# A woven delta-rule attention and feed-forward kernel: weight casts, one weight conversion and the transposes of the first chain in another order

## The chip, the cores and the metric

The kernel runs on one core of one Trainium2 chip. The metric is device time in microseconds of one execution; three runs of the kernel before gave a median of 634.15 us (633.36 to 634.79). The engines are named as the profile names them: PE (TensorE, with PEld for its weight loads), DVE (VectorE), ACT (ScalarE), POOL (GpSimd) and SP (SyncE, which here only issues DMAs).

## The reference

Per batch and head (4 x 8 of them) a 48 x 48 state is carried over 768 steps; the output of the attention is read before the state is updated. All heads side by side make a 3072 x 384 input of a feed-forward layer.

```python
k_n = k / (np.linalg.norm(k, axis=-1, keepdims=True) + 1e-06)
for t in range(S):                       # S = 768, D = 48, 4 x 8 heads
    y[:, :, t] = einsum('bhd,bhde->bhe', q[:, :, t], state)
    v_old = einsum('bhde,bhd->bhe', state, k_n[:, :, t])
    state = state + beta * einsum('bhd,bhe->bhde', k_n[:, :, t], v[:, :, t] - v_old)
x = y.transpose(0, 2, 1, 3).reshape(B * S, H * D)      # 3072 x 384
h = x @ w_in                                           # 384 x 2048
out = np.maximum(0.01 * h, h) @ w_out                  # 2048 x 384
```

## The kernel before

The 768 steps are cut into 12 blocks of 64. Within a block the recurrence is solved as a triangular system. The grams of keys and queries (pg, L289) are made on PE and scattered through memory (gs, gd, L). Then `inv` eliminates column by column on DVE: a product into tmp (L370) and an update of T (L375) per column. T starts with a memset (L397) and ends with a copy on ACT (L435); it is then sent out in pieces td and tt (L442, L443), which come back as operands of two merge products on PE, sq for pz and pu (L470) and rt. After these come pk (L598), pw (L615), pc (L625), and py (L635), which is the block's output; ACT copies it to ys (L637). Two groups (g = 0, 1) cover the four sequences.

`columns(n)` transposes ys into 384 x 256 columns on PE (px, L668), three pieces cc of 128 rows, and splits each into a high part xh (ACT, L119) and a low part xl (DVE, L120). `ffn(n)` runs over 16 chunks f of the 2048 middle columns: nine products into ph (L697: xh and xl with the high weights, xh with the low ones), gh and the rectified ph on ACT (L702, L703), the low part gl on DVE (L705), and later six products po (L687). The chunks alternate between two banks of PSUM, so that ph of chunk f comes after gl of chunk f-2. When a block is done, ACT copies po to ob and SP issues the stores to out (L732).

The weights come in as packed integers and are converted during blocks 0 and 1: per chunk an absolute value on ACT (L144), a clamp (L146), L150, L151 and L152 on DVE, a cast of the high part on ACT (L156), and the low part either on DVE (L169) or as products wl on PE (L175, L176).

The work of a block's solve, the next block's inverse and the feed-forward layer are woven together in the code, and then a scheduler orders the instructions of each engine by its own modelled times. `behind(name)` adds one constraint to it: the instruction is issued after the one marked with that name. A constraint in block 0 can therefore move instructions of later blocks. Each engine, and each DMA queue, does its instructions in order.

Of the kernel before, what the change touches and what calls it, by code (L numbers as in the profile page):

```python
# [9 lines left out]
F32 = mybir.dt.float32  # L10
# [13 lines left out]
TB = NSEQ * C  # L24
GS = 2
NGR = NSEQ // GS
# [5 lines left out]
P = 128  # L32
# [14 lines left out]
def delta_moe_kernel(ctx: ExitStack, tc, kq0, kqT, kv, qT, beta, cst, w_all, out, nblk):  # L47
# [10 lines left out]
    nc = tc.nc  # L58
    NFC, _, DO = w_all.shape[1:]
    NCC = DO // P  # L60
# [7 lines left out]
    ps_a = ctx.enter_context(tc.tile_pool(name="ps_a", bufs=4, space=PSUM))  # L68
# [20 lines left out]
    def of(x, n, g):  # L89
        return ring[x][(n * NGR + g) % NR[x]]  # L90
# [21 lines left out]
    raws, mark = {}, {}  # L112

    def behind(name):

        return tc.issue_after(mark[name]) if name in mark else nullcontext()

    def split(src, hi, lo):
        mark["xh"] = nc.scalar.copy(hi, src).ins  # L119
        return nc.vector.tensor_tensor(lo, src, hi.bitcast(F32), ALU.subtract)  # L120

    def load_w(f, gate=None):
        if f < NFC:
            raws[f] = raw = sb.tile([P, 2 * DO], U64, tag=f"w{f}", name=f"wr{f}", bufs=1)
            if gate:
                with behind(gate):
                    nc.vector.memset(raw[:, 0:1].bitcast(F32), 0.0)
            with behind("kq"):
                nc.sync.dma_start(raw, w_all[:, f].rearrange("p x n -> p (x n)"))
# [4 lines left out]
    def weights():  # L134

        for f in range(NFC):
            words = raws.pop(f).bitcast(U32).rearrange("p (n two) -> p two n", two=2)
            lo, hi = words[:, 0], words[:, 1]  # L140
            g = sb.tile([P, 2 * DO], F32, tag=f"c{f % 4}", name=f"cg{f}", bufs=1)
            gi = g.bitcast(U32)
            with behind("S" if f < KA else "xh"):
                nc.scalar.activation(g, hi.bitcast(F32), AF.Abs)  # L144
            with behind("mask" if f < 2 else "conv" if f == 2 else "x" if f < KA else f"gl{f - AG}" if f"gl{f - AG}" in mark else "x"):
                i = nc.vector.tensor_scalar(g, g, HI_MIN, HI_MAX, ALU.max, ALU.min)  # L146
            mark["work"] = i.ins
            if f + WAHEAD >= WEARLY:
                load_w(f + WAHEAD, "work")
            nc.vector.tensor_scalar(gi, gi, 3, 0x3FFFFFF8, ALU.logical_shift_left, ALU.bitwise_and)  # L150
            nc.vector.scalar_tensor_tensor(gi, hi, 0xC0000000, gi, ALU.bitwise_and, ALU.bitwise_or)  # L151
            i = nc.vector.scalar_tensor_tensor(gi, lo, 29, gi, ALU.logical_shift_right, ALU.bitwise_or)  # L152
            mark["conv"] = i.ins
            t = sb.tile([P, 4 * DO], F32R, tag=f"w{f}", name=f"w{f}", bufs=1)
            with behind("rv" if f < 2 else "xh"):
                nc.scalar.copy(t[:, 0:2 * DO], g)  # L156
            later.append((f, g, t))
            for y in range(2):
                for x, w in enumerate((wi, wo)):
                    w[y][f] = t[:, (2 * y + x) * DO:(2 * y + x + 1) * DO]  # L160
            yield
# [18 lines left out]
    Lh, gm, nrm, Tts, zs, ys, xs, done = {}, {}, {}, {}, {}, {}, {}, set()  # L180

    def need(gen, fn, n):
        while (fn, n) not in done:
            next(gen)
# [379 lines left out]
    def solve(n):  # L564
# [19 lines left out]
        def quarters():  # L584

            return ((c, u, e) for u in range(GU) for c in range(2) for e in range(2))
# [42 lines left out]
        def step_y(g):  # L629

            qa, v = of("q", n, g), of("v", n, g)
            pv = ps_a.tile([P, 512], F32, tag="a", name=f"py{n}_{g}")
            for c, u, e in quarters():
                a = (c ^ (u // NPAIR)) * C + e * HC
                nc.tensor.matmul(pv[a:a + HC, u * D:(u + 1) * D], qa[:, c, u, e * HC:(e + 1) * HC], v[:, c, u], start=True, stop=True)  # L635
            ys[n, g] = y = sb.tile([P, DO], F32, tag="ys", name=f"ys{n}_{g}", bufs=3)
            mark["ys"] = nc.scalar.copy(y, pv[:, 0:DO]).ins  # L637

        stages = [(0, load), (1, tie), (LD, kt), (LD + 1, step_w), (LD + 2, step_y), (LD + 3, step_s)]
        if n in (0, nblk - 1):  # L640
# [19 lines left out]
    def columns(n):  # L660

        need(sv, solve, n)
        xs[n] = parts = []
        px = [ps_a.tile([P, 2, TB], F32, tag="a", name=f"px{n}_{i}") for i in range(2)]
        part = [px[cc // 2][:, cc % 2] for cc in range(NCC)]
        for cc, x in enumerate(part):
            for g in range(NGR):
                i = nc.tensor.transpose(x[:, g * P:(g + 1) * P], ys[n, g][:, cc * P:(cc + 1) * P], eye)  # L668
        mark["px"] = i.ins
        for cc, x in enumerate(part):  # L670
            xh, xl = (sb.tile([P, TB], F32R, tag=t, name=f"{t}{n}_{cc}", bufs=3) for t in ("xh", "xl"))
            i = split(x, xh, xl)
            if not n:
                mark["x"] = i.ins
            parts.append((xh, xl))

    def ffn(n):
# [35 lines left out]
        if n + 1 < nblk:  # L713
            columns(n + 1)
# [69 lines left out]
KA, KB, WB = 4, 2, 12  # L784
IV, GG = ((7, 17), (6, 17), (6, 17), (2, 17)), ((0, 2), (1, 2), (1, 2))
LL, AG = 2, 6
# [67 lines left out]
```

## Time and profile before

| | before |
|---|---|
| median of 3 runs (lowest to highest) | 634.15 us (633.36 to 634.79) |
| span of the profiled execution | 633.8 us |
| busy PE, DVE, ACT | 590.5, 442.4, 331.1 us |
| mean granted clock of PE | 0.983 |
| share of the chain that ended last: PE, DVE | 81%, 11% |

The span is what the profiler saw from the first to the last instruction of one execution. A row of a timeline gives the start, the duration, the engine, the line, the operation and its operands; in square brackets stands the idle time of that engine just before, and what released it. A row with a count is a run of equal instructions. Instructions of one engine overlap by some hundredths of a microsecond, so spacings are taken from starts.

### The profile page before, as it was taken

What the parts mean: (1) busy time and instruction counts of PE and PEld (TensorE: products, weight loads), DVE (VectorE), ACT (ScalarE), POOL (GpSimd) and SP (SyncE); (2) the same over time, 40 slices, a digit from 0 to 9 for tenths busy, and PEclk for the clock granted to TensorE, in tenths of its full rate; (3) what the DMA queues carried; (4) which work ended last, traced back from release to release, by engine and by line L of the source; (5) the groups of instructions that cost most, each with busy time, mean ns of one, the idle gap of its engine ahead of it and who ended that gap; (6) DMA issues with size and microseconds to landing.
All of it is one profiled execution on the core that took longest, in us unless ns stands there. A gap on an engine that the chain in (4) does not pass through costs nothing.

```text
span 633.8 us, 22738 instructions
## 1 busy us (share of the span) xinstructions
PE 590.5 (93%) x9244; PEld 547.0 (86%) x9244; DVE 442.4 (70%) x1996; ACT 331.1 (52%) x855; POOL 10.7 (2%) x17
## 2 busy tenths in 40 slices
PE   5277999999989989999999999999999999999996
PEld 4265898988879989999999999999999999999996
DVE  3999999998747958759759759659669569221211
ACT  3465998634636446545546545545555545544332
POOL 6000000000000000000000000000000000000000
PEclk9986999999989999999999999999999999999999
DMA  6982973153156561453462561552571440500101
GB/s 124 302 261 79 252 248 77 24 113 52 27 105 135 113 115 37 90 103 72 93 119 54 102 143 21 99 122 46 102 155 28 88 102 4 87 24 3 26 1 26
DMA packets 124585, 59.72 MB, mean 94 GB/s; under 512 B 111424, under 2 KB 114624, under 8 KB 124480
## 3 DMA queue, kind: packets, MB, share of 16 engines
q1 hardware_dynamic: 121728, 57.28, 40.6%
q8 instruction: 73, 1.20, 0.8%
q10 hardware_dynamic: 2752, 0.98, 0.8%
q14 instruction: 32, 0.26, 0.2%
HBM read 46.96 MB, written 11.27 MB: 92 GB/s over the span
## 4 chain that ended last, share of the span: by engine, by line
PE 81%; DVE 11%; DMA 3%; SPq 2%; issue 2%; ACT 1%; DVEq 0%; ACTq 0%
PE ph L697 32%; PE po L687 30%; PE pk L598 3%; PE pg L289 3%; PE pw L615 3%; PE pc L625 3%; PE py L635 2%; DVE T L375 2%; DVE tmp L370 2%; PE wl L175 1%; DMA tt<-T 1%; PE px L668 1%; DVE cg L152 1%; PE pz L470 1%; PE pu L470 1%
## 5 line engine op out<-in xcount | busy, mean ns | idle before, releaser
L697 PE MATMUL ph<-xh,w 128*128 128x256 f32 x1152 | 246.6, 290 | 2.9 <-DVE gl L705 2.0
L697 PEld LDWEIGHTS ph<-xh,w 128*128 128x128 f32 x1152 | 192.1, 191 | 12.1 <-DVE gl L705 3.7
L687 PE MATMUL po<-w,gh 128*128 128x384 f32 x768 | 188.4, 343 | 3.1 <-ACT gh L702 3.1
L705 DVE TENSOR_TENSOR gl<-ph,gh 128x256 fp32r<-128x256 f32 x192 | 80.8, 421 | 150.7 <-ACT ph L703 148.8
L697 PE MATMUL ph<-xl,w 128*128 128x256 f32 x576 | 163.7, 286 | 1.0 <-DVE xl L120 1.0
L702 ACT ACTIVATE gh<-ph 128x256 fp32r<-128x256 f32 x192 | 73.7, 384 | 157.6 <-PE ph L697 145.2
L687 PEld LDWEIGHTS po<-w,gh 128*128 128x128 f32 x768 | 132.7, 189 | 7.5 <-ACT gh L702 5.3
L687 PE MATMUL po<-w,gl 128*128 128x384 f32 x384 | 116.5, 339 | 0.0
L370 DVE TENSOR_TENSOR tmp<-T,L 128x60 f32<-128x60 f32 (+35 forms) x661 | 111.6, 207 | 1.0
L375 DVE TENSOR_TENSOR T<-T,tmp 128x60 f32<-128x60 f32 (+35 forms) x661 | 111.5, 206 | 0.8
L697 PEld LDWEIGHTS ph<-xl,w 128*128 128x128 f32 x576 | 109.8, 191 | 2.5 <-DVE xl L120 1.7
L703 ACT ACTIVATE ph<-ph 128x256 f32<-128x256 f32 x192 | 73.3, 382 | 0.0
L687 PEld LDWEIGHTS po<-w,gl 128*128 128x128 f32 x384 | 67.1, 189 | 0.3 <-issue 0.2
L600 ACT ACTIVATE rt<-pk 48x512 f32<-48x512 f32 x44 | 26.1, 593 | 24.9 <-PE pk L598 24.1
L306 DVE TENSOR_TENSOR rq<-pg,csb 64x256 f32<-64x256 f32 x80 | 33.8, 423 | 4.0 <-ACT gs L293 2.6
L617 ACT COPY rv<-pw 64x384 f32<-64x384 f32 x48 | 22.7, 473 | 12.7 <-PE pw L615 11.9
L627 ACT COPY rv<-pc 48x384 f32<-48x384 f32 x44 | 20.8, 474 | 10.6 <-PE pc L625 10.1
L606 DVE TENSOR_TENSOR rv<-rv,nt 64x384 f32<-64x384 f32 x44 | 22.3, 553 | 0.6
L289 PE MATMUL pg<-kq 48*64 48x128 f32 x640 | 22.7, 275 | 0.0
L615 PEld LDWEIGHTS pw<-rv,rt 128*32 128x32 f32 x1536 | 19.2, 115 | 4.1 <-ACT gh L702 2.2
L615 PE MATMUL pw<-rv,rt 128*32 128x48 f32 x1536 | 21.6, 213 | 0.6 <-issue 0.6
L635 PEld LDWEIGHTS py<-rv,rq 128*32 128x32 f32 x1536 | 18.4, 112 | 4.2 <-ACT ph L703 2.3
(96 smaller groups left out, 542.6 us busy)
## 6 DMA issues: line engine op xcount, KB each, us to landing
wr<-in_w_all SPq DMA_DIRECT2D x16, 768.0 KB, 7.7
kq<-in_kqT SPq DMA_DIRECT2D x40, 192.0 KB, 4.1
L<-gd SPq DMA_DIRECT2D x20, 256.0 KB, 4.2
rk<-in_kv SPq DMA_DIRECT2D x24, 192.0 KB, 3.4
rv<-in_kv SPq DMA_DIRECT2D x24, 192.0 KB, 3.9
rq<-in_qT SPq DMA_DIRECT2D x24, 192.0 KB, 3.7
out<-ob SPq DMA_DIRECT2D x46, 96.0 KB, 2.3
td<-T SPq DMA_DIRECT2D x40, 64.0 KB, 2.9
```

The source lines that it names most:

```text
L289: nc.tensor.matmul(ps[b][c * 64:(c + 1) * 64, p * 128:(p + 1) * 128], kq[r, c ^ b, p, 0], kq[r, c ^ b, p].rearrange("p x t -> p (x t)"), s ...
L306: nc.vector.tensor_tensor(qa[DN, c, b * NPAIR:(b + 1) * NPAIR], pv[b][r, 1], tri[r].rearrange("p (o t) -> p o t", o=1).broadcast_to([C, NP ...
L370: nc.vector.tensor_tensor(tv, t[:, :, j:j + 1].broadcast_to([P, k, w]), L[:, j, j + 1:].rearrange("p (o w) -> p o w", o=1).broadcast_to([P ...
L375: mark["steps"] = nc.vector.tensor_tensor(t, t, tv, ALU.subtract).ins
L600: nc.scalar.mul(t[UP, c], pv[c * 64:c * 64 + D].rearrange("p (y v) t -> p y v t", y=2), -1.0)
L615: nc.tensor.matmul(pv[a:a + HC, u], t[:, c, u // NPAIR, u % NPAIR, e * HC:(e + 1) * HC], v[:, c, u], start=True, stop=True)
L635: nc.tensor.matmul(pv[a:a + HC, u * D:(u + 1) * D], qa[:, c, u, e * HC:(e + 1) * HC], v[:, c, u], start=True, stop=True)
L687: i = nc.tensor.matmul(po[t][:, :DO], a[:, ts_], w[f], start=(f == 0 and k == 0), stop=(f == NFC - 1 and k == 2))
L697: i = nc.tensor.matmul(ph, a[f][:, cc * P:(cc + 1) * P], x[cc][e], start=(k == 0), stop=(k == 3 * NCC - 1))
L702: nc.scalar.activation(gh, ph, AF.Prelu, alpha=0.01)
L703: i = nc.scalar.activation(ph, ph, AF.Prelu, alpha=0.01)
L705: i = nc.vector.tensor_tensor(gl, ph, gh.bitcast(F32), ALU.subtract)
```

## The change

Four places are edited, all in the chain from py of block 0 to its first chunks:

- The casts of the weights (L156) of chunks 0 and 1 no longer stand behind rv (the copies of pw, L617). That of chunk 0 stands behind the copy of y of group 0, that of chunk 1, like all later ones, behind the copy of x.
- The mark on the copy of y has the group in its name.
- The clamp of chunk 2 stands behind the last low part xl of block 0, where it stood behind the last step of the conversion before it.
- px of block 0 has three tiles, one for each cc, in three banks, and the six transposes run over g outside and cc inside. The other blocks keep two tiles, cc outside.

```diff
@@ -142,7 +142,7 @@
             gi = g.bitcast(U32)
             with behind("S" if f < KA else "xh"):
                 nc.scalar.activation(g, hi.bitcast(F32), AF.Abs)
-            with behind("mask" if f < 2 else "conv" if f == 2 else "x" if f < KA else f"gl{f - AG}" if f"gl{f - AG}" in mark else "x"):
+            with behind("mask" if f < 2 else "x" if f < KA else f"gl{f - AG}" if f"gl{f - AG}" in mark else "x"):
                 i = nc.vector.tensor_scalar(g, g, HI_MIN, HI_MAX, ALU.max, ALU.min)
             mark["work"] = i.ins
             if f + WAHEAD >= WEARLY:
@@ -152,7 +152,7 @@
             i = nc.vector.scalar_tensor_tensor(gi, lo, 29, gi, ALU.logical_shift_right, ALU.bitwise_or)
             mark["conv"] = i.ins
             t = sb.tile([P, 4 * DO], F32R, tag=f"w{f}", name=f"w{f}", bufs=1)
-            with behind("rv" if f < 2 else "xh"):
+            with behind("xh" if f else "ys0"):
                 nc.scalar.copy(t[:, 0:2 * DO], g)
             later.append((f, g, t))
             for y in range(2):
@@ -634,7 +634,7 @@
                 a = (c ^ (u // NPAIR)) * C + e * HC
                 nc.tensor.matmul(pv[a:a + HC, u * D:(u + 1) * D], qa[:, c, u, e * HC:(e + 1) * HC], v[:, c, u], start=True, stop=True)
             ys[n, g] = y = sb.tile([P, DO], F32, tag="ys", name=f"ys{n}_{g}", bufs=3)
-            mark["ys"] = nc.scalar.copy(y, pv[:, 0:DO]).ins
+            mark[f"ys{g}"] = nc.scalar.copy(y, pv[:, 0:DO]).ins
 
         stages = [(0, load), (1, tie), (LD, kt), (LD + 1, step_w), (LD + 2, step_y), (LD + 3, step_s)]
         if n in (0, nblk - 1):
@@ -661,10 +661,11 @@
 
         need(sv, solve, n)
         xs[n] = parts = []
-        px = [ps_a.tile([P, 2, TB], F32, tag="a", name=f"px{n}_{i}") for i in range(2)]
-        part = [px[cc // 2][:, cc % 2] for cc in range(NCC)]
-        for cc, x in enumerate(part):
-            for g in range(NGR):
+        k = 2 if n else 1
+        px = [ps_a.tile([P, k, TB], F32, tag="a", name=f"px{n}_{i}") for i in range(-(-NCC // k))]
+        part = [px[cc // k][:, cc % k] for cc in range(NCC)]
+        for cc, g in [(cc, g) for cc in range(NCC) for g in range(NGR)] if n else [(cc, g) for g in range(NGR) for cc in range(NCC)]:
+                x = part[cc]
                 i = nc.tensor.transpose(x[:, g * P:(g + 1) * P], ys[n, g][:, cc * P:(cc + 1) * P], eye)
         mark["px"] = i.ins
         for cc, x in enumerate(part):
```

The scheduler makes a new order from it. On ACT, in the first chain, the copies of pw, the casts of chunks 0 and 1, the two copies of y and the three copies xh stood in this order. In the changed kernel they are: the copies of pw, the copy of y of group 0, the cast of chunk 0, the copy of y of group 1, the three copies xh, the cast of chunk 1. On DVE the low weights of chunk 0 (L169) stay ahead of the three xl; those of chunk 1 and the conversion of chunk 2, which stood ahead of them, now follow them.

On DVE, in block 1, where the inverse T_1568 ends and the feed-forward chunks 4 to 8 run (in the changed kernel it is T_1569; T_2386 and T_2387 are the next; gl carries its chunk), before:

```order
L705 TENSOR_TENSOR gl_7_2424<-ph_73,gh_7_2423 128x256
L606 TENSOR_TENSOR rv_84<-rv_84,nt_2173 64x2x192 x2
L606 TENSOR_TENSOR rv_85<-rv_85,nt_2173 64x2x192
L350 SCALAR_TENSOR_TENSOR rc_2389<-rc_2389,L_2169 128x32
L606 TENSOR_TENSOR rv_85<-rv_85,nt_2173 64x2x192
L397 MEMSET T_2386 128x512
L705 TENSOR_TENSOR gl_8_2501<-ph_72,gh_8_2500 128x256
```

and in the changed kernel, from the end of the inverse on:

```order
L375 TENSOR_TENSOR T_1569<-T_1569,tmp_30_0_2119 128x8
L706 TENSOR_TENSOR gl_4_2291<-ph_72,gh_4_2290 128x256
L706 TENSOR_TENSOR gl_5_2344<-ph_73,gh_5_2343 128x256
L706 TENSOR_TENSOR gl_6_2364<-ph_72,gh_6_2363 128x256
L397 MEMSET T_2387 128x512
L346 TENSOR_SCALAR sr_2389<-L_2170 128x32
L347 TENSOR_SCALAR sr_2389<-sr_2389 128x32
L349 RECIPROCAL rc_2390<-sr_2389 128x32
L350 SCALAR_TENSOR_TENSOR rc_2390<-rc_2390,L_2170 128x32
L706 TENSOR_TENSOR gl_7_2425<-ph_73,gh_7_2424 128x256
L606 TENSOR_TENSOR rv_84<-rv_84,nt_2174 64x2x192
```

The memset of the next T stood behind gl of chunk 7 and the four L606; it now stands behind gl of chunk 6 and in front of gl of chunk 7. Earlier in the same stretch gl of chunk 2 has moved back by 16 instructions of the inverse (from row 370 of DVE's order to row 386), and gl of chunk 4 now comes after the inverse's last step where it stood 20 rows ahead of it.

On PE, in block 1, where pz of the block whose inverse has just ended comes in (ph_73 with w_1388 is chunk 11, with w_1301 chunk 9), before:

```order
L697 MATMUL ph_73<-xh_2_2076,w_1388 128x256
L697 MATMUL ph_73<-xl_2_2077,w_1388 128x256
L697 MATMUL ph_73<-xh_2_2076,w_1388 128x256
L687 MATMUL po_0_2133<-w_1300,gl_9_2539 128x384
L470 MATMUL pz_2312<-sq_2300,gm_1012 32x128 x8
L687 MATMUL po_1_2134<-w_1300,gl_9_2539 128x384
L687 MATMUL po_0_2133<-w_1377,gh_10_2646 128x384 x2
L687 MATMUL po_1_2134<-w_1377,gh_10_2646 128x384 x2
```

and in the changed kernel:

```order
L698 MATMUL ph_73<-xl_1_2074,w_1301 128x256
L698 MATMUL ph_73<-xh_1_2073,w_1301 128x256
L698 MATMUL ph_73<-xh_2_2077,w_1301 128x256
L470 MATMUL pz_2313<-sq_2301,gm_1013 32x128 x8
L698 MATMUL ph_73<-xl_2_2078,w_1301 128x256
L698 MATMUL ph_73<-xh_2_2077,w_1301 128x256
L688 MATMUL po_0_2134<-w_1181,gl_7_2425 128x384
L688 MATMUL po_1_2135<-w_1181,gl_7_2425 128x384
```

pz stood behind ph of chunk 11, among its po; it now stands inside ph of chunk 9, two products ahead of its end.

On SP, at the seam of blocks 1 and 2 (ob1 is the output of block 1, T_2386 or T_2387 the inverse for block 2's second product), before:

```order
L442 DMA td_3038<-T_2386 32x16x32 x2
L443 DMA tt_3039<-T_2386 1024x1x16
L540 DMA rk_76<-in_kv 64x768
L442 DMA td_3038<-T_2386 32x16x32
L540 DMA rk_77<-in_kv 64x768
L442 DMA td_3038<-T_2386 32x16x32
L732 DMA out<-ob_0_3011 64x384 x2
L732 DMA out<-ob_1_3015 64x384 x2
L443 DMA tt_3039<-T_2386 1024x1x16
L502 DMA sq_2302<-td_3038 32x8x32 x3
L499 DMA sq_2300<-tt_3039 32x8x32 x4
```

and in the changed kernel:

```order
L540 DMA rk_76<-in_kv 64x768
L540 DMA rk_77<-in_kv 64x768
L442 DMA td_3039<-T_2387 32x16x32 x2
L443 DMA tt_3040<-T_2387 1024x1x16
L442 DMA td_3039<-T_2387 32x16x32 x2
L443 DMA tt_3040<-T_2387 1024x1x16
L508 DMA rt_82<-td_3039 32x16x32
L508 DMA rt_83<-td_3039 32x16x32
L502 DMA sq_2303<-td_3039 32x8x32
L733 DMA out<-ob_0_3012 64x384 x2
L733 DMA out<-ob_1_3016 64x384 x2
L499 DMA sq_2301<-tt_3040 32x8x32 x4
```

All of td and tt now go ahead of the four stores of block 1, with two rt; the last tt stood behind the stores. The four sq<-tt stand behind the stores in both.

On PE, at the same seam, pz of block 2 stood behind ph of chunk 3 (w_964 and w_965 in the order's names); it now stands ahead of it, behind po of chunk 0.

## Rows read from the trace of the kernel before

**Rows 1.** The page's first part: busy time (share of the span) and instructions by engine.

```profile
PE 590.5 (93%) x9244; PEld 547.0 (86%) x9244; DVE 442.4 (70%) x1996; ACT 331.1 (52%) x855; POOL 10.7 (2%) x17
```

**Rows 2.** Stretches, one core: length, busy PE, PEld, DVE, ACT, POOL; granted clock; DMA.

```profile
240.00:250.00 10.00, 10.00 (x133) 9.26 (x131) 9.27 (x49) 6.19 (x16) 0.00 (x0) 1.00 0.10 17
```

**Rows 3.** The same view of three short stretches.

```profile
52.50:57.00 4.50, 2.38 (x9) 1.59 (x9) 4.34 (x6) 1.57 (x5) 0.00 (x0) 0.50 0.09 31
...
57.00:62.50 5.50, 5.50 (x18) 4.12 (x18) 5.10 (x12) 3.64 (x7) 0.00 (x0) 0.50 0.31 82
...
184.50:189.00 4.50, 4.35 (x32) 4.18 (x33) 3.64 (x11) 1.97 (x7) 0.00 (x0) 0.62 0.60 93
```

**Rows 4.** Timeline of ACT, first chain: start, duration, operation, count, [idle before <-releaser].

```profile
51.08 1.70 ACT L156 CAST w<-cg 128x768 fp32r<-128x768 f32 x2 [1.93 <-DVE cg L152]
...
52.80 0.86 ACT L637 COPY ys<-py 128x384 f32<-128x384 f32 x2
...
56.94 0.65 ACT L119 CAST xh<-px 128x256 fp32r<-128x256 f32 x2 [1.86 <-DVE xl L120]
```

**Rows 5.** Timeline of PE, first chain.

```profile
53.33 1.54 PE L668 MATMUL px<-csb,ys 128*128 128x128 f32 x6 [2.29 <-ACT ys L637]
...
56.96 0.58 PE L697 MATMUL ph<-xl,w 128*128 128x256 f32 x1 [1.04 <-DVE xl L120]
...
60.11 2.74 PE L175 MATMUL wl<-cg,csb 128*128 128x384 f32 x4
```

**Rows 6.** Timeline of DVE, first chain.

```profile
57.34 0.76 DVE L120 TENSOR_TENSOR xl<-px,xh 128x256 fp32r<-128x256 f32 x2 [0.44 <-ACT xh L119]
```

**Rows 7.** Timeline of PE, end of block 0.

```profile
110.20 0.39 PE L697 MATMUL ph<-xh,w 128*128 128x256 f32 x1 [0.26 <-DVE gl L705]
```

**Rows 8.** Timeline of DVE, block 1.

```profile
131.59 0.42 DVE L705 TENSOR_TENSOR gl<-ph,gh 128x256 fp32r<-128x256 f32 x1
...
140.23 0.17 DVE L375 TENSOR_TENSOR T<-T,tmp 128x8 f32<-128x8 f32 x1
...
142.62 1.50 DVE L606 TENSOR_TENSOR rv<-rv,nt 64x384 f32<-64x384 f32 x3
...
146.37 0.48 DVE L397 MEMSET T<- 128x512 f32 x1 [1.42 <-DMA tt<-T]
```

**Rows 9.** Timeline of PE, block 1.

```profile
142.14 0.28 PE L697 MATMUL ph<-xh,w 128*128 128x256 f32 x1
...
144.27 0.28 PE L697 MATMUL ph<-xh,w 128*128 128x256 f32 x1
...
147.36 0.39 PE L697 MATMUL ph<-xh,w 128*128 128x256 f32 x1 [0.81 <-DVE gl L705]
...
150.94 0.64 PE L470 MATMUL pz<-sq,gm 128*32 128x128 f32 x16
```

**Rows 10.** Timeline of SP's queue, block 1.

```profile
140.43 0.86 SPq L442 DMA_DIRECT2D td<-T  x2
...
146.41 2.03 SPq L499 DMA_DIRECT2D sq<-tt  x4
```

**Rows 11.** Timeline of PE, start of block 2.

```profile
172.91 0.51 PE L697 MATMUL ph<-xh,w 128*128 128x256 f32 x2 [0.56 <-ACT xh L119]
...
184.65 0.65 PE L470 MATMUL pz<-sq,gm 128*32 128x128 f32 x16 [2.48 <-ACT gh L702]
```

**Rows 12.** Timeline of ACT, start of block 2.

```profile
183.62 0.65 ACT L293 COPY gs<-pg 128x256 f32<-128x256 f32 x2 [5.84 <-DMA gd<-gs]
```

**Rows 13.** Timeline of SP's queue, start of block 2.

```profile
169.22 0.84 SPq L442 DMA_DIRECT2D td<-T  x2
...
174.34 2.44 SPq L732 DMA_DIRECT2D out<-ob  x4
...
180.74 2.03 SPq L499 DMA_DIRECT2D sq<-tt  x4
```

**Rows 14.** DMA issues from 160 to 190: operation, count, KB each, median us to landing.

```profile
sq<-tt SPq DMA_DIRECT2D x4, 32.0 KB, 2.3
```


## The prediction

> **What bounds the kernel now.** I read the page's busy times first: PE works 590.5 us of a span of 633.8 [rows 1], so only some 43 us are not PE's, and a change of order can win only from stretches in which PE waits or runs slowly. Then I read PE's busy time by stretches of ten microseconds. From 240 on every stretch looks like the one shown, PE busy 10.00 of 10.00 at clock 1.00 [rows 2]; whatever PE is early or late at 240 stands at the end. The question is therefore what the change does to PE up to 240, and I followed three places with the timelines: the first chain (50 to 63), the middle of block 1 (131 to 152), and the seam of blocks 1 and 2 (169 to 189). In each the reader is to see which engine PE waits for. In the first chain it is ACT's copy of y [rows 5], in block 1 DVE's gl [rows 9], at the seam ACT, which itself waits for DMAs [rows 11, 12].
>
> **The first chain.** Before, ACT does two casts (51.08, 1.70 together) and then the two copies of y (52.80, 0.86) [rows 4]; px waits 2.29 for them and starts at 53.33 [rows 5]. Now the copy of y of group 0 comes first. ACT was free for 1.93 before the casts [rows 4], so the copy no longer waits behind anything, and the second copy stands behind one cast of 0.85 instead of two: it is done near 51.08 + 0.85 + 0.43 = 52.4. The three transposes of group 1 (half of 1.54, so 0.77) then end near 53.2, where the last of the six ended at 54.87. The xh copies also wait less: the second of them waited 1.86 for DVE's xl, since pieces 0 and 1 share a tile [rows 4], and with three tiles it does not. The first xl of the remaining pair, at 57.34 [rows 6], moves to about 53.6.
>
> What hides it: DVE is busy 4.34 of the 4.50 us from 52.5 and 5.10 of the 5.50 from 57.0 [rows 3], and the work that stood ahead of xl (low weights of chunk 1, conversion of chunk 2) stands behind it now. PE starts ph some 1.7 us earlier and then finds the weights of chunk 2 not ready: wl started at 60.11 [rows 5], and the last step of that conversion now has the three xl, a second clamp, a low part and several steps for later chunks ahead of it; I place it near 62. PE fills most of that time with po of chunks 0 and 1, which stood later. So of the 1.7 us only what DVE itself gains stays: the 0.44 in which it waited for xh [rows 6] and a little more from steps that no longer wait for the one before. Bounds: nothing, or the 2.29 of PE's wait. At the end of block 0 PE waits for DVE again: ph of chunk 12 starts at 110.20 behind gl of chunk 10 [rows 7]. In the changed order one conversion step (about 0.9) stands behind that gl instead of ahead of it. I take 0.6 + 0.9 = 1.5 us early there.
>
> **The clock in the first chain.** Before, PE works from 52.5 to 62.5 at a granted clock of 0.50, after the waits for ACT and while it still waits for DVE [rows 3, 5]; by 64 it is nearly at full speed. PE's waits in the changed kernel are other ones but not fewer (chunk 1's low weights, then chunk 2's conversion), so I count the same slow stretch. A chunk's ph and po take 2.13 us at full clock (142.14 to 144.27) [rows 9] and as much again at half of it; half a chunk more or less in the slow stretch is 1.1 us either way, and that is part of the range.
>
> The Trainium skill, "TensorE: Matmul & The Clock Gate", Part 1, says that the slow state is the default and that activity releases it, so pieces of work between waits do not have to count as such. The trace agrees in that the clock stayed at 0.50 as long as px and the first ph came in pieces, and rose after the dense stretch from 57 [rows 3]. By this rule an earlier start that is followed by a new wait gives nothing back of the slow stretch.
>
> **Block 1.** The scheduler's new order puts the memset of the next T ahead of gl of chunk 7. That memset waits for the DMA of the T before it. Before, the inverse ended at 140.40, and the memset ran at 146.37, 5.97 later, after 1.42 of waiting on tt<-T [rows 8]; gl of chunk 7 was already done. Now the inverse ends earlier, because gl of chunks 4 and 5 (0.35 each of spacing) follow it and DVE is some 0.5 to 0.7 ahead: near 138.9 to 139. The same 5.97 later the memset runs at 144.9, 0.48 long, then four small steps of about 1 us, and gl of chunk 7 ends at 146.8. ph of chunk 9 must wait for it: 147.0, where it started at 144.27 [rows 9]. What is queued behind the memset on DVE is just that gl and the L606; who waits for them is PE.
>
> Next, pz now stands inside ph of chunk 9. It needs sq, whose four issues ran from 146.41 for 2.03 [rows 10], which with 2.3 to landing [rows 14] is 150.7; pz followed at 150.94 [rows 9]. With the inverse 1.4 earlier sq is there at about 149.3. So ph of chunk 9 is cut by a wait: 147.0, six or seven products until 147.9, pz at 149.3, its 0.57, the last two products and the six po. ph of chunk 10 comes near 151.0 instead of 147.36 [rows 9]. As pz (0.57) is done by then, and the wait of 0.81 that stood before chunk 10 is inside this, PE is about 2.6 us late from chunk 12 on. The lead of 1.5 is used up. Bounds: 1.0 late, if the tt of the other half were what the memset needs and it came 1.5 us earlier, or 4 late, if the L606 hold gl of chunk 8 as well.
>
> **The seam of blocks 1 and 2.** Here the kernel before loses most. SP sends td and tt from 169.22, then the four stores of block 1 (174.34, 2.44), then one tt, sq<-td, and the four sq<-tt at 180.74 for 2.03 [rows 13]. ACT's own DMAs wait on earlier ones, so its copies gs wait 5.84 and run at 183.62 [rows 12], with gh of chunk 3 behind them. PE waits 2.48 and starts pz at 184.65 [rows 11]. After that its clock is 0.62 in the mean of 4.50 us [rows 3]: at full speed this work would take 4.50 x 0.62 = 2.8, so 1.7 is lost. Together 4.2 us.
>
> In the changed order all td and tt, two rt and one sq go out before the stores, and the sq<-tt directly behind them. Shift PE by 2.6: it starts block 2 at 172.91 + 2.6 = 175.5. Ahead of pz it has ph of chunks 0 to 2, the grams and po of chunk 0, that is 182.17 - 172.91 (182.17 is 184.65 less the wait of 2.48) without chunk 3's ph and half of chunk 1's po, about three quarters of 2.13 or 1.6, so 7.7: it comes to pz at 183.2. The stores need the last po, 0.6 earlier than 175.5, and 0.9 of copies: 175.8; with 2.44 and 2.03 of issues and 2.3 to landing sq is there at 182.6. So sq is there just ahead of PE, PE waits little, and the clock stays up. ACT's DMAs wait on td, tt and rt that went out before the stores, so its gs copies come some 4 us earlier.
>
> PE then does pz (0.6), what it did from 185.3 to 189.0, now at full clock (3.7 x 0.62 = 2.3), and the work moved behind pz (1.6): 187.7, where before it was 189.0. So the 2.6 late turn into 1.3 early. I expect the next seam (216 to 240) to move along, since its inverse begins with the gs that now come earlier; I count it at zero, with 1.5 either way.
>
> **The sum.** 1.5 early, then 4.1 lost in block 1, then 3.9 won at the seam: 1.3 early. Span 633.8 - 1.3 = 632.5; the median of the runs is 0.35 above the span, so 632.8.
>
> **The rivals.**
> - *The block 1 wait stays, the seam doesn't get better.* pz at the seam waits for sq<-tt, which still go out behind the stores, and the stores wait for PE's last po. If ACT's DMAs still wait on a late one, or sq takes 2 us longer among the kq and rk loads, PE waits as long as before and the clock drops again. For it: 182.6 and 183.2 are close, so any delay becomes a wait. Against it: the last tt no longer stands behind the stores. It decides from a wait of about 2 us before pz, which brings the slow clock back. Then the 2.6 stand: 634.15 + 2.6 = 636.7, slower.
> - *The seam of blocks 2 and 3 takes it.* If PE there waits for DMAs and an inverse that don't start earlier, 1.3 early becomes about nothing: 634.1. For it: each seam so far is a chain of DMAs. Against it: its chain starts from the gs that move.
> - *The block 1 wait is not there.* If the memset's DMA lands with the gl before it, the lead of 1.5 stays, and the seam gives up to 4 less what the earlier PE must wait for sq, some 2 us: 634.15 - 3.3 = 630.9. For it: tt is sent as soon as the inverse ends. Against it: before, it took 5.97.
>
> **Chances and range.** The forecast 0.42, the slower rival 0.28, no change at the later seam 0.18, no wait in block 1 0.12. A run of this kernel can tell 0.2%, 1.3 us, from no change. The forecast's own range is 630.9 to 634.3; its middle lies at that bound, and as the seam's gain is the surer of its terms I give it 0.30 faster, 0.11 same and 0.01 slower. The third case is 0.14 same and 0.02 each way, the last all faster: faster 0.44, same 0.25, slower 0.31. The range that holds 8 of 10 goes from 630.2 to 636.9.
>
> **What would show it.** In the trace after: the last xh before 54; ph of chunk 12 of block 0 near 108.7; the memset in block 1 with an idle time of several us before it and gl of chunk 7 right behind; ph of chunk 9 near 147 and a wait of pz on sq inside it; at the seam ACT's gs without a wait of 5 us, pz near 183.5, and a clock of 1.00 from 180 to 190. Wrong would be: a slow clock at the seam again; a memset that doesn't wait; or PE busy less than 9.9 of ten after 240.

## The result, and the profile after

The change makes the kernel slower: 641.08 us in the median of four runs (639.94 to 644.11) against 633.75 (633.01 to 634.79) for the kernel before in the runs beside it; the ratio is 1.0116, with a 95% interval of 1.0088 to 1.0144. Forecast was 632.8, in a range of 630.2 to 636.9.

The profiled execution has a span of 638.1 us, 4.3 more than before, and a time of 639.94, the lowest of its four. In every run here the time is 1.7 to 1.9 us above the span. By that the profiled execution of before took some 635.6, which is above its median by more than 1. So the two profiles show some 4 of the 7 us. Their first parts (compare [rows 1]) show the same work:

```profile
PE 589.7 (92%) x9244; PEld 546.2 (86%) x9244; DVE 442.8 (69%) x1996; ACT 331.6 (52%) x855; POOL 10.7 (2%) x17
```

What differs is when PE waits. All of its waits between 125 and 245 us by engine and line (total, times, longest), before:

```profile
PE pz L470 <- ACT gh L702: 2.5, 1, 2.5
PE ph L697 <- DVE gl L705: 1.7, 3, 0.8
PE pz L470 <- DMA sq<-tt: 1.4, 1, 1.4
PE po L687 <- ACT gh L702: 0.7, 2, 0.4
PE ph L697 <- ACT xh L119: 0.6, 1, 0.6
PE pc L625 <- issue: 0.5, 1, 0.5
```

and after:

```profile
PE ph L698 <- DVE gl L706: 5.6, 4, 2.0
PE pz L470 <- ACT gs L293: 2.2, 1, 2.2
PE pz L470 <- DMA sq<-tt: 2.0, 2, 1.2
PE pc L625 <- issue: 1.5, 1, 1.5
PE po L688 <- ACT gh L703: 0.3, 1, 0.3
PE py L635 <- issue: 0.3, 1, 0.3
```

The wait for gl has grown by 3.9 us. To see where the time goes, I took the start of gh of one and the same chunk (ACT's first step after ph) in both traces; the difference is how late PE's feed-forward work is there, in us against the profile of before:

```
                              end of   start of  chunk 4   chunk 8   start of  chunk 7   chunk 12  start of  chunk 3  chunk 4
                              block 0  block 1   of 1      of 1      block 2   of 2      of 2      block 3   of 3     of 4
changed (first profile)        0.3      0.3       2.2       2.4       3.3       1.9       1.6       4.2       4.2      4.1
changed, second                0.1      0.1       2.0       2.2       2.4       1.1       0.7       3.4       3.4      2.8
changed, third                 0.3      0.3       2.3       2.8       3.0       2.8       2.5       5.2       5.2      4.4
changed, fourth                1.2      1.2       3.2       3.7       5.9       3.6       3.3       6.0       6.0      6.2
```

(From the last column on PE is full, as from 240 on before [rows 2], and the lateness stays.) Four steps are the same in all four profiles: nothing is gained in block 0, 2 to 3 us or more are lost in block 1, a part of that (0.5 to 2.6) is made good at the seam of blocks 1 and 2, and 2.6 to 2.8 are lost at the next seam.

In block 1 the timeline of PE shows the waits that answer to [rows 9]:

```profile
134.29 0.39 PE L698 MATMUL ph<-xh,w 128*128 128x256 f32 x1 [1.98 <-DVE gl L706]
...
138.04 0.39 PE L698 MATMUL ph<-xh,w 128*128 128x256 f32 x1 [1.01 <-DVE gl L706]
...
147.48 0.39 PE L698 MATMUL ph<-xh,w 128*128 128x256 f32 x1 [0.67 <-DVE gl L706]
...
149.36 0.64 PE L470 MATMUL pz<-sq,gm 128*32 128x128 f32 x16 [0.78 <-DMA sq<-tt]
...
151.32 0.28 PE L698 MATMUL ph<-xh,w 128*128 128x256 f32 x1
```

and that of DVE what they wait for (compare [rows 8]): gl of chunks 2 and 4, which come late behind the inverse, then the memset's wait, and gl of chunk 7 behind it.

```profile
133.81 0.42 DVE L706 TENSOR_TENSOR gl<-ph,gh 128x256 fp32r<-128x256 f32 x1
...
139.69 0.42 DVE L706 TENSOR_TENSOR gl<-ph,gh 128x256 fp32r<-128x256 f32 x1
...
145.72 0.48 DVE L397 MEMSET T<- 128x512 f32 x1 [3.05 <-DMA tt<-T]
...
147.01 0.42 DVE L706 TENSOR_TENSOR gl<-ph,gh 128x256 fp32r<-128x256 f32 x1
```

At the seam of blocks 1 and 2 the rows that answer to [rows 3, 11 to 13] are, on PE, ACT and SP and in the stretch's clock:

```profile
186.04 0.64 PE L470 MATMUL pz<-sq,gm 128*32 128x128 f32 x16 [2.18 <-ACT gs L293]
```
```profile
185.66 0.65 ACT L293 COPY gs<-pg 128x256 f32<-128x256 f32 x2 [4.60 <-DMA gd<-gs]
```
```profile
178.64 3.42 SPq L733 DMA_DIRECT2D out<-ob  x4
182.10 2.11 SPq L499 DMA_DIRECT2D sq<-tt  x4
```
```profile
184.50:189.00 4.50, 2.96 (x31) 2.48 (x31) 0.00 (x0) 1.05 (x4) 0.00 (x0) 1.00 0.63 97
```

ACT still waits for its DMAs, and PE for ACT, nearly as long as before; but the granted clock stays at 1.00 where it was 0.62, and that is the part made good in this profile. It is not the change's own gain. A second profile of the kernel before has 1.00 in the same stretch, and the third of the changed kernel has 0.62 in the 4.5 us that follow its pz:

```profile
184.50:189.00 4.50, 4.50 (x54) 3.85 (x43) 3.73 (x11) 1.51 (x5) 0.00 (x0) 1.00 0.56 87
```
```profile
185.77:190.27 4.50, 4.35 (x32) 4.18 (x33) 1.04 (x3) 1.86 (x7) 0.00 (x0) 0.62 0.54 84
```

At the next seam ph of chunk 15 waits for gl of chunk 13, which stands in DVE's order behind the inverse's last steps:

```profile
225.42 0.39 PE L698 MATMUL ph<-xh,w 128*128 128x256 f32 x1 [1.93 <-DVE gl L706]
```
```profile
224.74 0.17 DVE L370 TENSOR_TENSOR tmp<-T,L 128x8 f32<-128x8 f32 x1
224.94 0.42 DVE L706 TENSOR_TENSOR gl<-ph,gh 128x256 fp32r<-128x256 f32 x1
```

Before, that inverse ended at 220.6 and gl of chunk 13 ran at 222.24, after DVE had waited 1.63 for ACT. Now gh of chunk 13 is made at 219.99, 1.5 earlier than before, and its gl stands behind the inverse. The inverse is late because it began late: its memset ran at 200.76 instead of 196.16. It did not wait for its input, since the two loads of L had landed by 194.95 (193.29 before). It stands directly behind gl of chunk 6, as before, and that gl came late. On PE pk, which stood behind ph of chunk 6 (pk at 194.63, gh of chunk 6 at 193.68), now stands inside it, two products ahead of its end, and ACT's copies of pk (197.12, 2.45) go ahead of gh of chunk 6 (199.59). PE and DVE after:

```profile
195.97 1.99 PE L598 MATMUL pk<-rt,rk 64*48 64x64 f32 x64
197.89 0.39 PE L698 MATMUL ph<-xl,w 128*128 128x256 f32 x1
```
```profile
200.28 0.42 DVE L706 TENSOR_TENSOR gl<-ph,gh 128x256 fp32r<-128x256 f32 x1 [3.38 <-ACT ph L704]
200.76 0.48 DVE L397 MEMSET T<- 128x512 f32 x1
```

and DVE before, where gl of chunk 6 did not have to wait:

```profile
195.68 0.42 DVE L705 TENSOR_TENSOR gl<-ph,gh 128x256 fp32r<-128x256 f32 x1
196.16 0.48 DVE L397 MEMSET T<- 128x512 f32 x1
```

### The profile page after: what moved, and what is told of

Same layout as the page of the kernel before. It is cut to its first block, busy times and chain, and to the rows that moved or that the text cites. A ratio compares the mean times of both kernels' runs of the same rounds, so it can differ in the third digit from the quotient of the medians.

```text
span 638.1 us, 22736 instructions
## 1 busy us (share of the span) xinstructions
PE 589.7 (92%) x9244; PEld 546.2 (86%) x9244; DVE 442.8 (69%) x1996; ACT 331.6 (52%) x855; POOL 10.7 (2%) x17
## 4 chain that ended last, share of the span: by engine, by line
PE 79%; DVE 12%; DMA 3%; issue 2%; ACT 2%; SPq 2%; DVEq 0%; ACTq 0%
PE ph L698 30%; PE po L688 29%; PE pk L598 3%; DVE T L375 3%; DVE tmp L370 3%; PE pg L289 3%; PE pw L615 3%; PE pc L625 3%; PE py L635 2%; PE wl L175 2%; PE px L669 1%; DMA sq<-tt 1%; PE pz L470 1%; PE pu L470 1%; DVE rq L306 1%
## 5 line engine op out<-in xcount | busy, mean ns | idle before, releaser
L703 ACT ACTIVATE gh<-ph 128x256 fp32r<-128x256 f32 x192 | 73.7, 384 | 151.5 <-PE ph L698 147.4
L375 DVE TENSOR_TENSOR T<-T,tmp 128x60 f32<-128x60 f32 (+35 forms) x661 | 112.7, 208 | 0.8
L370 DVE TENSOR_TENSOR tmp<-T,L 128x60 f32<-128x60 f32 (+35 forms) x661 | 112.0, 208 | 0.9
L617 ACT COPY rv<-pw 64x384 f32<-64x384 f32 x48 | 22.8, 474 | 11.5 <-PE pw L615 10.7
L606 DVE TENSOR_TENSOR rv<-rv,nt 64x384 f32<-64x384 f32 x44 | 22.4, 555 | 0.6
```

The costliest lines, as they stand in the source:

```text
L370: nc.vector.tensor_tensor(tv, t[:, :, j:j + 1].broadcast_to([P, k, w]), L[:, j, j + 1:].rearrange("p (o w) -> p o w", o=1).broadcast_to([P ...
L375: mark["steps"] = nc.vector.tensor_tensor(t, t, tv, ALU.subtract).ins
L703: nc.scalar.activation(gh, ph, AF.Prelu, alpha=0.01)
```

## The experiments

Ratios are to the kernel before, run beside each on the same chip, with 95% intervals. "Steps" are the L370 and L375 of the inverse that ends in block 1. The first two put the question whether DVE's order in block 1 is the cause, one from each side.

**gl put back ahead of the steps, in the changed kernel.** The helper `after_in_queue` adds issue order only; the lists give the steps (column, half) that go behind gl of a chunk:

```diff
+FIRST = {2: ((22, 0), (24, 1)), 3: ((23, 0), (25, 1)), 4: ((26, 0), (27, 1)), 5: ((29, 0),)}
 ...
             mark["gl"] = mark[f"gl{f}"] = i.ins
+            if n == 1:
+                for a, y in FIRST.get(f, ()):
+                    after_in_queue(steps[1, a, y, 0], f"gl{f}")
```

> The changed kernel with one thing added: in block 1 the inverse's steps stand behind gl of chunks 2 to 5 again, as in the kernel before (issue order on DVE only). First chain as changed. Theory (the loss is DVE's order in block 1: gl behind 16 and more steps of the inverse, and what follows from it at the two seams): ratio to before 0.996 to 1.003, PE between 130 and 140 busy about 9.1 of 10 again instead of 7.0, block 2 starts within 1 us of before's 172.9. Rival (the loss comes from the first chain and the weights' conversions, or from the stores and pieces of T on SP): the ratio stays 1.008 to 1.015.

Measured: 634.46 us (634.18 to 636.14, ten runs), ratio 1.0004 (0.9993 to 1.0015). The loss is gone, with all four edits in place. PE's stretches from 130 to 150:

```profile
130.00:140.00 10.00, 9.66 (x63) 8.69 (x63) 9.65 (x49) 2.64 (x8) 0.00 (x0) 1.00 0.62 131
140.00:150.00 10.00, 9.66 (x67) 9.01 (x67) 8.03 (x34) 4.18 (x11) 0.00 (x0) 1.00 0.44 62
```

where the changed kernel has

```profile
130.00:140.00 10.00, 7.01 (x47) 6.36 (x46) 9.61 (x57) 1.51 (x5) 0.00 (x0) 1.00 0.59 125
140.00:150.00 10.00, 8.55 (x72) 7.80 (x70) 5.01 (x15) 3.36 (x9) 0.00 (x0) 1.00 0.51 74
```

Block 0 ends 1.8 us late in this profile, so the first chain gained nothing, and block 2 starts 0.4 us later than before instead of 2.4 to 5.9. In this version the scheduler, left free, also puts the memset back behind gl of chunk 7, pz into the end of ph of chunk 11, and in block 2 pk behind ph of chunk 6. So the run shows that the loss lies in the later order and not in the first chain; it takes away the whole train of displacements, not the gl alone.

**gl held behind the steps, in the kernel before.**

```diff
+LAST = {2: (27, 1, 1), 3: (30, 1, 1), 4: (30, 0, 1)}
 ...
-            i = nc.vector.tensor_tensor(gl, ph, gh.bitcast(F32), ALU.subtract)
+            with tc.issue_after(steps[1, *LAST[f]]) if n == 1 and f in LAST else nullcontext():
+                i = nc.vector.tensor_tensor(gl, ph, gh.bitcast(F32), ALU.subtract)
```

> The kernel before, none of the four edits, with gl of chunks 2, 3 and 4 in block 1 held behind the steps of the inverse behind which the changed kernel has them. Theory (DVE's order in block 1 is the cause): ratio 1.006 to 1.015, ph of chunk 4 waits about 2 us for gl of chunk 2, block 2 starts 2.5 to 3.5 us late, and 4 us late after the seam of blocks 2 and 3. Rival (the first chain or SP): within 0.3% of before.

Measured: 637.3 us (636.75 to 638.09), ratio 1.0052 (1.0034 to 1.0071), just below what the theory expected and clear of the rival. Block 1 loses the same 2.0 us by chunk 4 as in the changed kernel:

```profile
130.00:140.00 10.00, 7.02 (x46) 6.31 (x46) 9.63 (x57) 2.12 (x7) 0.00 (x0) 1.00 0.55 115
```

but block 2 starts only 1.3 us late, not 2.5 to 3.5, and the end is 2.3 late. The order in block 1 alone, with nothing changed in the first chain, makes about half of the loss. It is not gl alone here either: with gl held, the scheduler also puts the memset in front of gl of chunk 7 and pz inside ph of chunk 9, as in the changed kernel:

```profile
145.33 0.48 DVE L405 MEMSET T<- 128x512 f32 x1 [1.92 <-DMA tt<-T]
...
145.77 0.41 DVE L714 TENSOR_TENSOR gl<-ph,gh 128x256 fp32r<-128x256 f32 x1
```

The order in block 2 is that of the kernel before.

**The memset alone**, from three sides. In the changed kernel, put back behind gl of chunk 7:

```diff
+            if n == 1 and f == 7:
+                after_in_queue(steps["T", 2], "gl7")
```

> The changed kernel with only the memset of T in block 1 held behind gl of chunk 7, as in the kernel before; gl of chunks 2 to 4 stay behind the steps of the inverse. If the loss is those three gl: ratio to before 1.007 to 1.012, ph of chunk 4 still waits about 2 us. If it is the memset that waits for the DMA in front of gl of chunk 7: 0.999 to 1.004.

Measured: 642.78 us (641.04 to 643.67), ratio 1.0146 (1.0107 to 1.0185), above both ranges: nothing is won. In this order pz of block 1 waits 2.29 for sq. Then with gl put back as in the first experiment and the memset kept early:

```diff
+            with tc.issue_after(steps["T", 2]) if n == 1 and f == 7 else nullcontext():
+                i = nc.vector.tensor_tensor(gl, ph, gh.bitcast(F32), ALU.subtract)
```

> The changed kernel with gl of chunks 2 to 5 ahead of the inverse's steps as before, and the memset of T in front of gl of chunk 7 as changed. If the memset's wait by itself makes a part of the loss that lasts: 1.003 to 1.008. If it is only the three gl: 0.998 to 1.002.

Measured: 641.83 us (640.13 to 643.37), ratio 1.0125 (1.0088 to 1.0163), more than either side expected. And the same two lines, without gl put back, in the kernel before:

> The kernel before with only the memset of T in block 1 put in front of gl of chunk 7. If the memset's wait is enough by itself: 1.003 to 1.008, ph of chunk 9 waits 1 to 2 us for gl of chunk 7. If it costs only with the changed first chain: 0.998 to 1.002.

Measured: 637.02 us (634.88 to 638.19), ratio 1.0044 (1.0029 to 1.0058). The memset stands in front of gl and waits for the DMA:

```profile
146.63 0.48 DVE L405 MEMSET T<- 128x512 f32 x1 [2.73 <-DMA tt<-T]
147.03 0.36 DVE L714 TENSOR_TENSOR gl<-ph,gh 128x256 fp32r<-128x256 f32 x1
```

The scheduler puts pz inside ph of chunk 9 here too. So in the kernel before the memset's displacement, with that of pz, costs 0.44%; the version with gl held has these two and the gl, and costs 0.52%. What gl adds by itself is not shown: the two intervals overlap, and no run holds gl alone. In the changed kernel undoing the memset alone, or the gl alone, gives nothing back; but both of these versions keep the changed order in block 2, and the version without loss does not.

**pz held behind ph of chunk 11**, in the changed kernel, PE's order only:

```diff
+            if n == 1 and f == 11:
+                for m in steps.get(("pz", 2), ()):
+                    after_in_queue(m, "ph")
```

> The changed kernel with only pz of block 1 held behind ph of chunk 11 on PE, so that it does not stand in front of the end of ph of chunk 9; DVE's order up to gl of chunk 10 as changed. If DVE's order alone makes the loss: 1.009 to 1.013, as the changed kernel. If pz's wait in the middle of ph of chunk 9 (0.78 us there) starts the rest: 1.003 to 1.008.

Measured: 638.37 us (636.61 to 639.87), ratio 1.0072 (1.0049 to 1.0094), in the second range. By that the wait of pz inside ph of chunk 9 would be some 0.3 to 0.4% of the loss, but this is not shown: the interval overlaps those of the changed kernel, all later placements move with the edit, and in the one profile block 1 loses 2.7 us from start to start, against 2.4 to 4.7 in the four of the changed kernel.

**Parts of the change.** Five of the six subsets, made of the lines of the diff. The clamp alone:

```diff
-            with behind(... "conv" if f == 2 else "x" if f < KA else ...):
+            with behind(... "x" if f < KA else ...):
```

> Only the clamp of chunk 2 behind the last xl; casts and px as before. In the order of DVE gl of chunk 2 in block 1 has 37 steps of the inverse between it and gl of chunk 1 (23 before, 39 changed). Theory: ratio 1.005 to 1.015 with the wait of ph of chunk 4 near 2 us. Rival (the first chain's casts and px make the loss): within 0.4% of before.

Measured: 644.45 us (643.22 to 645.45), ratio 1.0163 (1.0141 to 1.0186). The ratio is at the upper edge of the theory's range, but the place is another: most of it is lost in the first chain. Block 0 ends 9.0 us late, and PE's busy time there, in the stretch that was full before (20.00), is

```profile
60.00:80.00 20.00, 13.85 (x162) 10.19 (x162) 18.78 (x31) 10.29 (x17) 0.00 (x0) 0.88 0.65 195
```

It then stands 11 us late at the start of block 3.

Casts and px without the clamp:

> Casts and px as changed, the clamp of chunk 2 as before. In the order of DVE there are 23 steps between gl of chunks 1 and 2 in block 1, as before. Theory: no loss in block 1, ratio 0.995 to 1.002, the first xh near 53. Rival (the first chain's casts and px make the loss): ratio 1.006 or more.

> Casts and px without the clamp again, in more rounds: 0.996 to 0.999 if the first reading (0.9979) was right; 0.999 to 1.002 if it was the chip.

Measured: 632.77 us, ratio 0.9979 (0.9966 to 0.9993), and measured again, in twelve runs, 632.79, 0.9977 (0.9965 to 0.9988). This order keeps gl of chunk 2 where it was, block 0 ends 0.3 and 1.1 us early in the two profiles, and at the seam of blocks 1 and 2 the clock stays up, as it did in one of the two profiles of the kernel before:

```profile
180.00:190.00 10.00, 8.72 (x80) 7.23 (x79) 4.23 (x12) 4.92 (x15) 0.00 (x0) 1.00 0.68 123
```

Casts and clamp without px:

> Casts and clamp as changed, px as before (two tiles, pieces outside). In the order of DVE block 1 has 23 steps of the inverse between gl of chunks 1 and 2, as the kernel before and as the one with casts and px. Theory (DVE's order in block 1 decides): 0.996 to 1.003. Rival (the clamp costs by itself in the first chain, as it did alone): 1.008 to 1.016.

Measured: 635.84 us with a wide spread (632.55 to 640.54), ratio 1.0033 (1.0005 to 1.0061), at the upper edge of the first expectation and far from the second. With the casts moved, the clamp's place no longer costs 9 us in block 0, but 1.7.

Casts alone (the two lines on L155 and L637), and px alone:

> Only the casts moved. By the account that the clamp's move costs and the rest gains a little: no loss in block 0, gl of chunk 2 in block 1 23 steps behind that of chunk 1 as before, ratio 0.996 to 1.001. If px's three tiles are what gained with the casts: 0.999 to 1.003.

> Only px of block 0 in three tiles and by groups. ACT still does both casts before the copies of y, so px starts as before at 53.3; only the wait of xh for xl (1.86) goes. Account as above: 0.998 to 1.002, and the end of block 0 within 0.5 us of before.

Measured: casts 632.25 us (630.78 to 634.61), ratio 0.997 (0.9955 to 0.9985); px 637.01 (635.21 to 637.77), ratio 1.0038 (1.0025 to 1.0052), a miss of the expectation: block 0 ends 0.4 us late, and the seam of blocks 2 and 3 loses 2.9 more. The casts alone beat both kernels, and are no worse than casts and px; the two intervals overlap.

**The changed kernel again**, once in four runs and twice in a single execution with its profile, and the kernel before in a single execution:

> The changed kernel again, for a second profile: three kernels with its order in block 0 were 1.0 to 2.7 us late at the end of block 0, where its own profile was 0.3 late. If its first chain varies from execution to execution: late by 0.3 to 2.7 at gh of chunk 15 of block 0 and about 3 us more at the start of block 2; ratio 1.009 to 1.014. If its profile was typical: 0.3 late at block 0's end again.

> A look at the changed kernel. If the part of the loss that its two profiles don't show is in the first chain: gh of chunk 15 of block 0 is 1 to 3 us late against the profile of before in executions of 640 us and more, with a lower clock between 50 and 65. If it is elsewhere: 0.1 to 0.3 late as in the first two.

> As the look before it: one more execution of the changed kernel, read at the end of block 0 and at the start of blocks 2 and 3.

> A look at the kernel before: its first profile (635.6 us) lies at the slow end of its runs. If its first chain varies as that of the changed kernel does, block 0 ends up to 2 us earlier or later than there; if what differs is later, block 0 ends within 0.3 us.

Measured: 640.44 us (638.55 to 641.14), ratio 1.0101 (1.008 to 1.0122), and the single executions 640.19 and 641.87; the kernel before 635.31. The table above has the four profiles: block 0 ends 0.1, 0.3, 0.3 and 1.2 us late, so in one of four a further microsecond is lost there, and the rest of the spread arises in block 1. The second profile of the kernel before ends 0.6 us early against its first, and at 635.31 lies again above its median of 634.28. Of the 3 us by which the medians differ more than the first two profiles do, 1.8 is the profile of before lying above its median (635.6 to 633.75), and 1.1 that of the changed kernel lying below its own (639.94 to 641.08).

**The order in block 2** was not changed by itself in any run, but the eighteen profiles sort by it. In eleven of them pk stands inside ph of chunk 6: the four of the changed kernel, the three versions of it with the memset put back, the memset kept early or pz put back, and the parts px, casts and px (both profiles), casts and clamp. All eleven lose 1.4 to 3.0 us between chunk 12 of block 2 and the start of block 3, with a wait of PE of 1.0 to 2.3 there. In the seven others pk stands behind that ph: the kernel before (both profiles), its versions with gl held and with the memset early, the changed kernel with gl put back, the casts alone and the clamp alone. None of the six that can be set against the first loses anything there (from 1.1 won to nothing), and no wait of PE there is over 0.4. The casts and px have this order too and are still faster than the kernel before, since they come to chunk 12 of block 2 3.1 and 4.3 us early; so this order has a price at that seam, and what it is worth in all is not shown.

## Why the prediction was wrong

By the first profile, the four terms of the sum came out as 0.3 us late instead of 1.5 early at the end of block 0, 3.0 lost in block 1 instead of 4.1, 1.7 won at the seam of blocks 1 and 2 instead of 3.9, and 2.6 lost at the next seam, which had been counted at nothing. The misses are 1.8, -1.1, 2.2 and 2.6 us.

- *"I take 0.6 + 0.9 = 1.5 us early there"* (end of block 0): failed in size and sign of what is left. The first chain itself moved as worked out: the first xh at 52.45 (the last was forecast before 54), xl at 52.85, ph at 52.87, then waits for chunk 1's low weights, gl and chunk 2's conversion. ACT's and PE's rows after:

```profile
52.45 0.93 ACT L119 CAST xh<-px 128x256 fp32r<-128x256 f32 x3 [0.42 <-PE px L669]
```
```profile
52.87 0.39 PE L698 MATMUL ph<-xh,w 128*128 128x256 f32 x1 [0.24 <-ACT xh L119]
...
55.80 0.51 PE L698 MATMUL ph<-xh,w 128*128 128x256 f32 x2 [1.01 <-DVE w L169]
...
60.56 0.62 PE L688 MATMUL po<-w,gl 128*128 128x384 f32 x2 [1.70 <-DVE gl L706]
```

  The head start of 2.3 us goes in waits of 1.01 and 1.70 and a wl that starts at 61.52 instead of 60.11. The term that failed is the wait at chunk 12 [rows 7]: gl of chunk 10 did come 1.0 us earlier, but ph of chunk 12, forecast at 108.7, started without a wait at 110.57 (PE's timeline after):

```profile
110.57 0.28 PE L698 MATMUL ph<-xh,w 128*128 128x256 f32 x1
```

  It was 110.20 before. PE was full from 80 on (its stretch after), and what it had lost between 50 and 80 was work that still lay ahead of that ph:

```profile
80.00:110.00 30.00, 30.00 (x571) 26.14 (x570) 29.17 (x56) 28.47 (x56) 0.00 (x0) 1.00 0.54 167
```

  I let gl, on which the last wait there had ended, set the start of that ph; but PE, which had to do the work ahead of it, had become the bound.

- *The clock in the first chain*: not the same slow stretch. From 50 to 60 the granted clock was 1.00 in the mean in the first profile after, against 0.62 before, and PE gained nothing by it, because it waited for DVE. It was slow later, behind the wait of 1.70: 0.50 from 62.50 to 64.00, where it was 0.94 before. So the conclusion that an earlier start with a new wait behind it gives nothing back of the slow stretch did not hold for the clock from 50 to 60, in which PE was busy 6.80 of 10.00 in pieces. PE's stretches after:

```profile
50.00:60.00 10.00, 6.80 (x94) 5.26 (x93) 9.76 (x19) 5.82 (x12) 0.00 (x0) 1.00 0.36 108
62.50:64.00 1.50, 1.50 (x7) 0.42 (x9) 1.50 (x3) 0.05 (x1) 0.00 (x0) 0.50 0.21 86
```

  The forecast had allowed for this within its 1.1 us either way.

- *Block 1*: right for the memset, nearly in time, but with one wait left out. gl of chunk 7 was forecast to end at 146.8, ph of chunk 9 to start at 147.0, chunk 10 at 151.0; it was 147.4, 147.48 and 151.32. The memset's wait, forecast to last until 144.9, lasted until 145.72. "About 2.6 us late" stands against 3.3 at the start of block 2 (2.4 to 5.9 in four profiles). The figures named for it, 151.0 less 147.36 less 0.57, give 3.1, and the lead of 1.5 was not there. What was left out is gl of chunk 2: it was read as moved behind 16 more steps and given no price, and by chunk 4 PE had lost 1.9 us to it. That the sum came near is in part luck: with the memset alone moved, in the kernel before, block 1 loses 2.7 us, so the two waits do not add.

- *"So sq is there just ahead of PE, PE waits little"* at the seam (forecast 3.9 won): failed for the wait. The order of td, tt and the stores on SP did change as read, yet ACT's gs waited 4.60 for its DMAs and PE 2.18 for ACT, against 5.84 and 2.48. The stores were placed at 175.8; they began at 178.64, after ACT's copies to ob (until 177.75) and behind td, tt, rt and one sq<-td on the same queue (until 178.60), and took 3.42 instead of 2.44, so the last sq<-tt landed at 185.90 and not at 182.6. *"ACT's DMAs wait on td, tt and rt that went out before the stores"* failed with it. By the trace's records of issues, landings and semaphores each gd<-gs after the first was issued 0.02 us after the landing of the SP transfer for which it waited: a store at 183.09 and two sq<-tt at 184.19 and 185.29 (before, a tt at 180.53, an sq<-td at 181.56 and an sq<-tt at 183.25). So ACT stood behind the very transfers that it was to overtake. PE's wait ended with ACT's first gs at 186.04, 0.14 after the last sq<-tt had landed; without ACT it would have been about as long. ACT's issues after:

```profile
181.10 4.53 ACTq L297 DMA_DIRECT2D gd<-gs  x4
```

  The 1.7 us of the clock were won in this profile, 3.3 late becoming 1.6 late, but that is luck: 0.5 was won in the third profile of the changed kernel, and the kernel before won 1.2 there in its second profile against its first, with nothing changed.

- *"I expect the next seam (216 to 240) to move along, since its inverse begins with the gs that now come earlier"*, counted at zero: failed, by 2.6 us (from 1.6 to 4.2 late), and this is the largest miss; with the three steps before it alone PE would have been 1.6 late. The gs came 2.0 later (185.66 to 183.62), and the inverse does not begin when they allow it: its memset stands behind gl of chunk 6 in DVE's order and ran 5.8 us after L was there (2.9 before). I had read PE's order in block 2 only as far as pz. gl of chunk 5 was 1.3 late, that of chunk 6, with pk inside its ph, 4.6, the memset behind it as much, and behind the inverse came gl of chunk 13 (2.7 late) and pz at 239.96 (4.1 late).

- *The baseline*: I took the median to be 0.35 above the span of the same execution. Each run here shows 1.7 to 1.9, and the profiled execution was one of the slower.

- The slower rival, "the block 1 wait stays, the seam doesn't get better", had 0.28 and 636.7; it is nearest in time, with too small a price, since it held the loss to block 1's and had no term for the seam after. The second rival, with 0.18, named that seam, and an inverse there that does not start earlier; but it took back only the 1.3 that had been forecast.

Why the pieces in block 1 don't add is settled only in part. With the memset put back, or gl put back and the memset kept early, or pz put back, the chip shows 1.46%, 1.25% and 0.72%; all three keep the changed order in block 2 and lose 2.6, 2.7 and 1.7 us at the seam behind it, where the version with gl put back loses nothing. The scheduler also places other later work anew in each, and no run here holds all later placements fixed.

## What to carry to other kernels

Where a scheduler orders the whole program, an edit in the first chain is also an edit of every later order; count what it moves on the busiest in-order queue, above all an instruction that waits for a DMA and comes to stand in front of one that the critical engine waits for, or steps of a long serial chain put ahead of it. A constraint that keeps the later order while one edit is tried (here a few lines of issue order) tells the edit's own worth from that of the shuffle: here 1.0004 against 1.0116. The new order has to be read to the end of the stretch in which the critical engine still waits, not only at the places that lost most before: here the seam that was counted at nothing lost 2.6 us, behind an order that the forecast had not read. A clock that differs between executions of one order is not a gain of the order.

## What had not been expected of the hardware

One and the same order of block 0 (the changed kernel's four profiles and the four versions that differ from it only later) started py between 47.0 and 49.6 us, with mean granted clocks of 0.53 to 0.66 from 40 to 50. A later start was not a later end: py at 48.74 ended block 0 0.1 us late, py at 47.16 ended it 1.8 late. So the clock in that stretch differs between executions by more than the effects that were sought, and one profile of the first chain settles nothing under a microsecond. The seam of blocks 1 and 2 is the same: in the 4.5 us from about its pz on the kernel before ran at 0.62 in one execution and 1.00 in the other, behind waits of 2.48 and 1.46 us, and the changed kernel at 1.00, 1.00, 0.62 and 1.00, behind waits of 2.18, 2.20, 2.35 and 1.02.

A DMA issue can stand behind a transfer of another queue with which it shares no data. In the trace each gd<-gs on ACT waits on the semaphore that its own landing will raise, and that an earlier transfer of SP, such as a store of out, raised last. In all eighteen profiles the copies gs at that seam stand behind such issues, after 3.3 to 6.2 us of idle time of ACT.
